# Leaving softmax rows undivided and multiplying the attention output by inverse row sums instead

## The chip, the cores and the metric

The kernel runs on one core of a Trainium2 chip. The metric is the device time of one execution in microseconds (us); lower is better. The engines are TensorE (PE in the profile; PEld is its weight load), VectorE (DVE), ScalarE (ACT), GpSimd (POOL) and SyncE (SP), which issues the DMA transfers.

## The reference

Three blocks in a row: an attention with a decay bias, a mixture of four experts with relu, and a gated feed-forward block.

```python
scores = (1 / sqrt(D)) * q @ k.T              # B=2, H=8, S=576, D=64
cum = cumsum(maximum(s, 0))
bias = -(cum[:, None] - cum[None, :])
scores = where(causal, -1e9, scores + minimum(bias, 0))
attn = exp(scores - max(scores))
attn = attn / (sum(attn) + 1e-9)
x = (attn @ v) as [1152, 512]                 # heads side by side
p = domain_probs / (sum(domain_probs) + 1e-9)
x = sum over e of p[:, e] * (maximum(x @ w1[e], 0) @ w2[e])      # 4 experts, F = 1024
g = x @ w_gate                                # F = 1536
out = ((g * sigmoid(g)) * (x @ w_val)) @ w_out
```

## The kernel before

**One program, ordered by a planner.** The Python code creates tasks (`add`, or `any_of` where one of several engines may do it) with an engine, an estimated cost, the tasks they depend on, a rank, and the buffers they take and give back (`Ring`). `Plan.step` takes again and again the ready task that can start first by these estimates, with the lower rank winning a tie, and writes its instructions down. So the order on each engine is fixed when the program is built, and each engine works through its own list in that order. A task that may run on several engines (letters `v`, `a`, `p` for DVE, ACT, POOL) goes to the one with the best estimated end.

**Attention.** A unit is a pair of heads and a group of query blocks of 128 rows: 16 pairs in all. The first eight pairs hold query blocks 0 and 1 and are computed in plain fp32 (four chains each); the last eight hold blocks 2, 3 and the half block 4, in split precision (five chains each, since block 4 has 64 rows and takes both heads at once). That makes 72 chains. A chain is:

- `scores` (tag `sp`): the score matmuls, line L599;
- `least`: mask and row minimum of the negated scores into the tile `ns`, on DVE, L608;
- `exp`: on ACT, L615, with the row sums as a by-product in column 2 of the small tile `st`;
- `guard`: two DVE instructions on 128x1, add 1e-9 (L620) and reciprocal (L621);
- `norm`: `ns` times the inverse sum, row by row, on POOL or DVE (L314, the body of `scale`);
- `turn`: TensorE transposes `ns` into the bank `tp`, L645; `copy`: ACT or DVE moves it to `p`, L304 or L306.

After the chains of a pair, `products` (L695) multiplies by v into the bank `po`, whose rows are the two heads' 64 dimensions and whose columns are tokens. `values` then writes `po` to `xh` (rounded, `high`) and the rest to `xl` (`low`, L711). There are five `ns` buffers, two `sp` banks, two `tp` banks and one `po` bank.

**What lies beside attention.** The four pairs with query blocks 0 and 1 of the first batch fill the first 256 tokens of x. As soon as they are done, the planner may also hand out the expert block ("dense" work): matmuls into the bank `h` (lines L1036 to L1038, three for each product in split precision), into `o` (L1196 to L1198), their evacuations on ACT and DVE, and the preparation of weights (a cast on ACT, `wah` or `woh`, and a subtraction on POOL, `wal` or `wol`, L317). While attention runs, a job covers 256 or 512 tokens of one expert's slice (`jobs`, list `part`), with eight products where the later form of the same work (`seven`, L1134 to L1136) needs seven. Where TensorE would have nothing in the estimate, a filler transposition is written (L404). The jobs handed out by the end of attention are all done in the plain form; the form with seven products begins after them, and its sums of x are made by `sums_of_x`.

## Time and profile before

| What | Before |
|---|---|
| Runs | 3976.26, 752.39 and 751.43 us (median 752.39) |
| Profiled execution | 750.75 us |
| Its span, first to last instruction | 748.9 us |
| Busy: PE, PEld | 722.3 us (96%), 628.7 us (84%) |
| Busy: DVE, ACT, POOL | 615.1 (82%), 374.8 (50%), 442.8 us (59%) |
| Mean granted TensorE clock, as a share of full | 0.995 |
| Last value product of attention (L695) | up to 156.5 us |
| First product in the form with seven (L1134) | 212.7 us |

The shares of a whole span hide the stages. Attention, alone or with early dense work beside it, fills the first 157 us; then come the rest of the early jobs, and from about 213 us the long stretch of expert and feed-forward products. In a timeline a matmul's duration includes its latency: the distance from one start to the next is what it costs TensorE in a row of them.

### The profile page before, as it was taken

To read this page: it belongs to the slowest core of one execution; us is meant where nothing else is said; L and a number is where in the kernel's file an instruction comes from. 1 tells how busy PE (TensorE), PEld (TensorE's weight loads), DVE (VectorE), ACT (ScalarE), POOL (GpSimd) and SP (SyncE) were. 2 spreads that over 40 slices of the span, in tenths; PEclk is the share of its full clock that TensorE was granted. 3 is DMA by queue.
4 is the path that set the end of the run, shared out by engine and by line. 5 is a ranking of instruction groups with operands and counts; after the bars stand their busy time and mean duration, and the time that the engine had idled before them with its cause. 6 is when DMAs were issued, how large, how long until landed. Compare 5 with 4: busy or idle time off the path is not lost.

```text
span 748.9 us, 12443 instructions
## 1 busy us (share of the span) xinstructions
PE 722.3 (96%) x4332; PEld 628.7 (84%) x4332; DVE 615.1 (82%) x1251; ACT 374.8 (50%) x845; POOL 442.8 (59%) x440
## 2 busy tenths in 40 slices
PE   7999999999999998999999999999899999999997
PEld 6767766778788897989889898899798999999996
DVE  7688886769988988889977989779897788787765
ACT  4999786845435454545635455365642423243210
POOL 5345543489744466655565574579886676676321
PEclk8999999999999999999999999999999999999999
DMA  5557532003454234442445344202210101010003
GB/s 115 122 134 213 153 93 58 29 1 113 155 188 166 91 136 144 141 157 92 141 141 169 93 155 134 99 29 93 77 57 29 57 30 57 29 57 1 1 1 126
DMA packets 77230, 72.57 MB, mean 97 GB/s; under 512 B 45976, under 2 KB 56280, under 8 KB 77168
## 3 DMA queue, kind: packets, MB, share of 16 engines
q1 hardware_dynamic: 77168, 71.78, 31.2%
q8 instruction: 34, 0.56, 0.3%
q14 instruction: 28, 0.23, 0.1%
HBM read 59.82 MB, written 11.80 MB: 96 GB/s over the span
## 4 chain that ended last, share of the span: by engine, by line
PE 64%; DVE 17%; DMA 7%; issue 5%; ACT 4%; SPq 1%; POOL 0%; DVEq 0%; POOLq 0%; ACTq 0%
PE h L1134 9%; PE h L1136 9%; PE h L1135 9%; PE o L1196 8%; PE o L1197 8%; PE o L1198 8%; DMA hh<-in_moe_w_val 3%; PE sp L599 3%; PE po L695 2%; PE tp L645 2%; DVE cc L1153 2%; DMA hh<-in_moe_w_out 2%; DVE hl L804 2%; DVE ns L608 2%; DMA hh<-in_moe_w_gate 1%
## 5 line engine op out<-in xcount | busy, mean ns | idle before, releaser
L1196 PE MATMUL o<-woh,hh 128*128 128x512 f32 x396 | 157.0, 396 | 5.3 <-DVE acc_b L1280 2.9
L1153 DVE TENSOR_TENSOR cc<-cc,h 128x320 f32<-128x320 f32 (+1 forms) x288 | 127.1, 450 | 38.6 <-PE h L1136 30.9
L1198 PE MATMUL o<-woh,hl 128*128 128x512 f32 x396 | 155.1, 392 | 3.0 <-POOL hl L317 1.9
L1197 PE MATMUL o<-wol,hh 128*128 128x512 f32 x396 | 155.8, 393 | 0.0
L317 POOL TENSOR_TENSOR wal<-raw,wah 128x512 fp32r<-128x512 f32 (+1 forms) x56 | 71.5, 1290 | 42.1 <-ACT wah L304 42.1
L1134 PE MATMUL h<-xh,wsh 128*128 128x320 f32 (+1 forms) x320 | 95.2, 298 | 0.7 <-ACT cc L304 0.7
L1136 PE MATMUL h<-xh,wsl 128*128 128x320 f32 (+1 forms) x320 | 95.0, 297 | 0.0
L1135 PE MATMUL h<-xl,wsh 128*128 128x320 f32 (+1 forms) x320 | 94.9, 297 | 0.0
L1198 PEld LDWEIGHTS o<-woh,hl 128*128 128x128 f32 x396 | 74.4, 188 | 21.2 <-POOL hl L317 2.8
L1196 PEld LDWEIGHTS o<-woh,hh 128*128 128x128 f32 x396 | 74.5, 188 | 19.8 <-DVE acc_b L1280 4.6
L317 POOL TENSOR_TENSOR hl<-cc,hh 128x512 fp32r<-128x512 f32 (+1 forms) x29 | 41.7, 1436 | 75.4 <-ACT hh L1256 70.1
L317 POOL TENSOR_TENSOR wol<-raw,woh 128x512 fp32r<-128x512 f32 x52 | 75.0, 1453 | 16.1 <-ACT woh L304 16.0
L1197 PEld LDWEIGHTS o<-wol,hh 128*128 128x128 f32 x396 | 74.5, 188 | 10.8
L1253 ACT ACTIVATE cc<-cc 128x640 f32<-128x640 f32 (+1 forms) x48 | 33.3, 694 | 99.6 <-DVE cc L1153 99.6
L314 POOL TENSOR_SCALAR ns<-ns,st 128x256 f32<-128x256 f32 (+4 forms) x62 | 33.6, 544 | 64.1 <-DVE st L621 14.5
L1134 PE MATMUL h<-xh,wah 128*128 128x256 f32 (+1 forms) x240 | 71.1, 296 | 0.0
L1136 PE MATMUL h<-xh,wal 128*128 128x256 f32 (+1 forms) x240 | 71.0, 296 | 0.0
L1135 PE MATMUL h<-xl,wah 128*128 128x256 f32 (+1 forms) x240 | 71.0, 296 | 0.0
L1134 PEld LDWEIGHTS h<-xh,wsh 128*128 128x128 f32 x320 | 60.4, 189 | 2.6 <-ACT cc L304 1.1
L1135 PEld LDWEIGHTS h<-xl,wsh 128*128 128x128 f32 x320 | 60.5, 189 | 1.4
L1136 PEld LDWEIGHTS h<-xh,wsl 128*128 128x128 f32 x320 | 60.5, 189 | 0.0
L1280 DVE SCALAR_TENSOR_TENSOR acc_b<-o,pr,acc_b 128x512 f32<-128x512 f32 x75 | 55.4, 742 | 5.1 <-PE o L1198 4.8
(156 smaller groups left out, 1823.0 us busy)
## 6 DMA issues: line engine op xcount, KB each, us to landing
raw<-in_moe_w SPq DMA_DIRECT2D x40, 512.0 KB
n<-hl SPq DMA_DIRECT2D x36, 256.0 KB
raw<-n SPq DMA_DIRECT2D x18, 512.0 KB
hh<-in_moe_w_gate SPq DMA_DIRECT2D x12, 512.0 KB
hh<-in_moe_w_val SPq DMA_DIRECT2D x12, 512.0 KB
hh<-in_moe_w_out SPq DMA_DIRECT2D x12, 512.0 KB
kr<-in_k SPq DMA_DIRECT2D x24, 128.0 KB
qr<-in_q SPq DMA_DIRECT2D x24, 128.0 KB
```

What stands on the lines that cost most here:

```text
L314: {"v": nc.vector, "p": nc.gpsimd}[e].tensor_scalar(to, x, by, 1.0, op0=ALU.mult, op1=ALU.mult)
L317: {"v": nc.vector, "p": nc.gpsimd}[e].tensor_tensor(to, x, f32(y), op=ALU.subtract)
L599: nc.tensor.matmul(sp[:, :s1 - s0], Q[:m, h, x0:x0 + P], K[:m, h, s0:s1], start=x == 0, stop=x == len(todo) - 1)
L1134: nc.tensor.matmul(hp, wh, h, start=c == 0, stop=False)
L1135: nc.tensor.matmul(hp, wh, l, start=False, stop=False)
L1136: nc.tensor.matmul(hp, wl, h, start=False, stop=c == 1)
L1153: nc.vector.tensor_tensor(part(k), part(x), banks[i], op=ALU.add)
L1196: nc.tensor.matmul(op, hh[:, f, ts], wh[:, f, :], start=f == 0, stop=False)
L1197: nc.tensor.matmul(op, hh[:, f, ts], wl[:, f, :], start=False, stop=False)
L1198: nc.tensor.matmul(op, hl[:, f, ts], wh[:, f, :], start=False, stop=f == NF - 1)
L1253: nc.scalar.activation(src()[:, o], src()[:, o], AF.Relu)
L1280: nc.vector.scalar_tensor_tensor(acc(t), bank_(), sc, acc(t), op0=ALU.mult, op1=ALU.add)
```

## The change

The rows of `ns` are no longer divided by their sums. `guard` and `norm` are gone from all 72 chains, and `turn` waits for `exp` alone. `exp` leaves its sum in a tile `sums` that a pair shares (a column for each chain). Once for each pair, two DVE instructions make the inverses of all columns (`inverse`); `spread` copies each column over 64 columns of a tile `inv_w` (POOL or DVE; 256 columns, and for the half block `spread_last` writes two 64x64 corners); `rows_of` turns `inv_w` on TensorE into a `tp` bank, so that the inverse of a token stands in its column for the 64 rows of its head (for the half block a matmul with `twin`, two identity halves added); `keep` copies this to a tile `R`; `product` multiplies the bank `po` by `R` into `R` on DVE; `high` and `low` make `xh` and `xl` from `R` instead of from `po`. There are four `ns` buffers in place of five. Besides, the tile `dps` is no longer there (`pr` is used), and the sums of x of the second half get a rank behind the preparation of the weights.

```diff
-NS = 5
+NS = 4
-NORM = "pv"
...
+        inv_w = ap.tile([P, 3, P], F32, name="inv_w", bufs=1)
+        twin = ap.tile([P, D], F32, name="twin", bufs=1)
+
+        def halves():
+            nc.gpsimd.memset(inv_w[:, 2], 0.0)
+            nc.gpsimd.tensor_tensor(twin, ident[:, :D], ident[:, D:], op=ALU.add)
+        t_own = add("pool", 0.6, halves, [t_id], rank=11)
...
-                box["st"] = ap.tile([P, 6], F32, name="st", tag="st", bufs=8)
+                box["st"] = ap.tile([P, 2], F32, name="st", tag="st", bufs=6)
...
-                    ns, ns, AF.Exp, bias=st[:, len(spans) - 1:len(spans)], scale=-1.0, accum_out=st[:, 2:3])
-
-            def guard():
-                st = box["st"]
-                nc.vector.tensor_scalar(st[:, 4:5], st[:, 2:3], 1.0e-9, None, op0=ALU.add)
-                nc.vector.reciprocal(st[:, 5:6], st[:, 4:5])
-
-            def norm(on):
-                ns = box["ns"][:, :w]
-                scale(on, ns, ns, box["st"][:, 5:6])
+                    ns, ns, AF.Exp, bias=st[:, len(spans) - 1:len(spans)], scale=-1.0, accum_out=ch.sum(qb, heads))
...
-            tG = inorder("g", add("dve", 0.21, guard, [tE, before.get("g")], rank=i + RANK["g"]))
-            tN = inorder("n", any_of(NORM, "scale", w, norm, [tG, before.get("n")], rank=i + RANK["n"]))
+            ch.exps.append(tE)
...
-                tT = inorder("t", add("pe", (c1 - c0) * pe(2 * P), turn, [tN, before.get("t")],
+                tT = inorder("t", add("pe", (c1 - c0) * pe(2 * P), turn, [tE, before.get("t")],
...
+                def inverse():
+                    m = 2 * nf + (nf < len(self.qbs))
+                    box["inv"] = self.sums[:, 1, :m]
+                    nc.vector.tensor_scalar(self.sums[:, 0, :m], self.sums[:, 0, :m], 1.0e-9, None, op0=ALU.add)
+                    nc.vector.reciprocal(box["inv"], self.sums[:, 0, :m])
+
+
+                def spread(on):
+                    to = inv_w[:, :nf].rearrange("p b (h d) -> p (b h) d", h=2)
+                    move(on, to, box["inv"][:, :2 * nf].unsqueeze(2).to_broadcast([P, 2 * nf, D]))
+
+                def spread_last(on):
+                    for x in half:
+                        move(on, inv_w[x, nf, x], box["inv"][x, 2 * nf:].to_broadcast([D, D]))
+
+                def rows_of():
+                    box["r"] = ps.tile([P, BANK], F32, name="tp", tag="tp", bufs=2)
+                    for x in range(len(self.qbs)):
+                        a, m = x * P, min(P, n - x * P)
+                        if m == P:
+                            nc.tensor.transpose(box["r"][:, a:a + m], inv_w[:, x], ident)
+                        else:
+                            nc.tensor.matmul(box["r"][:, a:a + m], inv_w[:, x], twin, start=True, stop=True)
+
+                def keep(on):
+                    box["R"] = ap.tile([P, 320], F32, name="R", tag="R", bufs=1)[:, :n]
+                    move(on, box["R"], box["r"][:, :n])
+
+                def product():
+                    nc.vector.tensor_tensor(box["R"], self.po[:, :n], box["R"], op=ALU.mult)
+
                 def high(on):
-                    move(on, xh[:, hp, dst], self.po[:, :n])
-
-                def low():
-                    nc.vector.tensor_tensor(xl[:, hp, dst], self.po[:, :n], f32(xh[:, hp, dst]), op=ALU.subtract)
+                    move(on, xh[:, hp, dst], box["R"])
+
+                def low(on):
+                    minus(on, xl[:, hp, dst], box["R"], xh[:, hp, dst])
+                r = i + RANK["f"]
+                tI = add("dve", 0.38, inverse, list(self.exps), rank=i + RANK["g"])
+                tW = [any_of("pv", "copy", 2 * nf * D, spread, [tI], take=[ring("iw", 1)], rank=i + RANK["g"])]
...
+                tR = inorder("t", add("pe", nf * pe(2 * P) + (len(self.qbs) - nf) * pe32(D), rows_of, tW + [before.get("t"), t_own],
+                                      take=[ring("tp")], give=[(tW[0], ring("iw"))], rank=i + RANK["g"]))
+                tK = any_of(COPY, "bank", n, keep, [tR], take=[ring("R", 1)], give=[(tR, ring("tp"))], rank=i + RANK["g"])
...
-                tX = any_of(FOLD, "bank", n, high, [tV], rank=i + RANK["f"])
-                done_x[g].append(add("dve", dve(n), low, [tX], give=[(tV, ring("po", 1))], rank=i + RANK["f"]))
+                tF = add("dve", dve(n), product, [tV, tK], give=[(tV, ring("po", 1))], rank=r)
+                tX = any_of("av", "copy", n, high, [tF], rank=r)
+                done_x[g].append(any_of("vp", "two", n, low, [tX], give=[(tK, ring("R"))], rank=r))
...
+        rank = WRANK + made["n"] - 2 if t0 else prompt() + 1
...
-        dps = ap.tile([P, NT, E], F32, name="dps", bufs=1)
+        dps = pr
```

The planner orders the changed program anew, and dense work moves. In TensorE's list the last value product stands behind 120 dense matmuls before the change and behind 162 after it; the jobs handed out by the end of attention are four before and six after. The first place is TensorE's list at the eighth pair, the last one in plain fp32 (`sp` scores, `tp` transposes of `ns`, `h` first transposes of k with `kr` and then dense products of `xh` and `wah`, `po` the value product). Before the change:

```order
L599 MATMUL sp<-kb_111,qb_115 128x64
L508 MATMUL h<-ident,kr 128x128 x4
L645 MATMUL tp<-ident,ns 128x128 x2
L1036 MATMUL h<-xh,wah 128x256
L1037 MATMUL h<-xl,wah 128x256
L1038 MATMUL h<-xh,wal 128x256
...
L695 MATMUL po<-p,vr 64x256 x2
L695 MATMUL po<-p,vr 64x128 x2
L645 MATMUL tp<-ident,ns 128x128 x3
```

After it, at the same pair (the lines have other numbers: L607 was L599, L516 was L508, L643 was L645, L700 was L695, L1248 to L1250 were L1196 to L1198; L737 is `rows_of`):

```order
L1248 MATMUL o<-woh,hh 128x512
L1249 MATMUL o<-wol,hh 128x512
L1250 MATMUL o<-woh,hl 128x512
...
L607 MATMUL sp<-kb_111,qb_115 128x64
L700 MATMUL po<-p,vr 64x256 x2
L700 MATMUL po<-p,vr 64x128 x2
L516 MATMUL h<-ident,kr 128x128 x4
...
L737 MATMUL tp<-ident,inv_w 128x128 x2
L643 MATMUL tp<-ident,ns 128x128 x3
```

Twelve dense matmuls, the four products of `h` just ahead, stand before this pair's value product before the change; after it there are 51, and the second matrix of the first job (`o`) has begun.

The second place is the end of attention on TensorE, the last pair, before the change:

```order
L1038 MATMUL h<-xh,wal 128x512
L645 MATMUL tp<-ident,ns 128x128 x7
L1196 MATMUL o<-woh,hh 128x512
L1197 MATMUL o<-wol,hh 128x512
L1198 MATMUL o<-woh,hl 128x512
...
L695 MATMUL po<-p,vr 64x320 x6
L695 MATMUL po<-p,vr 64x192 x2
L695 MATMUL po<-p,vr 64x64 x2
```

And after it:

```order
L643 MATMUL tp<-ident,ns 128x128 x7
L1248 MATMUL o<-woh,hh 128x512
L1249 MATMUL o<-wol,hh 128x512
L1250 MATMUL o<-woh,hl 128x512
L737 MATMUL tp<-ident,inv_w 128x128 x2
L739 MATMUL tp<-twin,inv_w 128x64
L700 MATMUL po<-p,vr 64x320 x6
L700 MATMUL po<-p,vr 64x192 x2
L700 MATMUL po<-p,vr 64x64 x2
```

`rows_of` now stands directly ahead of the value product. At four of the last eight pairs it stands ahead of it, here and at two others with nothing or one short block between; at the other four it stands behind it.

The third place is POOL's list, from the seventh pair on (`wal` and `wol` are the weight subtractions, `kb` a copy of k), before the change:

```order
L317 TENSOR_TENSOR wal<-raw,wah 128x512 x2
L314 TENSOR_SCALAR ns<-ns,st 128x256
L314 TENSOR_SCALAR ns<-ns,st 128x128
L314 TENSOR_SCALAR ns<-ns,st 128x256
L314 TENSOR_SCALAR ns<-ns,st 128x384
L308 TENSOR_SCALAR kb_113<-ka_112 64x512
```

And after it:

```order
L316 TENSOR_TENSOR wal<-raw,wah 128x512 x2
L316 TENSOR_TENSOR wol<-raw,woh 128x512 x2
L307 TENSOR_SCALAR inv_w<-sums 128x256
L316 TENSOR_TENSOR wal<-raw,wah 128x512 x2
L307 TENSOR_SCALAR kb_113<-ka_112 64x64
```

The multiplications of `ns` are gone, a spread stands where a pair ends, and the weight subtractions follow one another.

## Rows read from the trace of the kernel before

**Rows 1.** Windows by stretch: length, PE, PEld, DVE, ACT, POOL busy, clock, DMA, GB/s.

```profile
12.00:48.00 36.00, 34.22 (x216) 25.34 (x217) 23.71 (x140) 32.50 (x122) 14.29 (x30) 0.91 0.50 114
48.00:84.00 36.00, 33.95 (x235) 25.80 (x236) 32.92 (x113) 33.61 (x96) 19.88 (x25) 1.00 0.65 176
84.00:157.00 73.00, 69.89 (x433) 50.48 (x433) 50.95 (x176) 50.76 (x141) 32.61 (x44) 1.00 0.27 71
157.00:213.00 56.00, 54.46 (x272) 46.49 (x271) 54.78 (x77) 27.17 (x58) 44.01 (x41) 1.00 0.37 118
213.00:744.00 531.00, 521.34 (x3138) 472.71 (x3136) 441.83 (x732) 227.59 (x426) 324.39 (x276) 1.00 0.28 91
```

**Rows 2.** Chain of waits, shares by line, of 12 to 48, 48 to 84, 84 to 157 us.

```profile
by line: PE sp L599 30.0%; PE tp L645 14.8%; PE h L508 9.4%; PE po L695 8.9%; DMA dps<-in_moe_domain_probs 5.4%; PE o L404 4.2%; ACT ns L615 3.9%; issue 3.6%; DVE ns L608 3.5%; SPq L1522 3.3%; SPq L1520 2.7%; POOL ns L314 2.1%; SPq L450 1.8
...
by line: DVE ns L608 18.2%; DVE ka L551 9.5%; PE tp L645 8.4%; DVE ns L314 7.8%; DVE qb L554 7.2%; ACT ka L304 6.8%; PE po L695 6.5%; issue 5.7%; PE sp L599 4.2%; PE h L508 3.6%; ACT ns L615 3.5%; ACT wah L304 2.9%; DVE st L621 2.9%; DVE p 
...
by line: PE po L695 16.1%; PE sp L599 14.7%; PE tp L645 11.5%; PE h L508 6.1%; DVE ns L608 5.5%; PE h L1036 5.0%; PE h L1038 4.5%; PE h L1037 4.5%; ACT p L304 4.2%; PE o L1196 3.8%; ACT ns L615 3.8%; DVE ka L551 3.8%; PE o L1197 2.9%; PE o 
```

**Rows 3.** Groups by line and shape, 0 to 157 us: count, busy, mean, idle before.

```profile
L621 DVE RECIPROCAL st<-st 128x1 f32<-128x1 f32 x72 | 11.8, 164 | 2.5
L620 DVE TENSOR_SCALAR st<-st 128x1 f32<-128x1 f32 x72 | 10.7, 148 | 8.6 <-ACT ns L615 8.1
L304 ACT COPY p<-tp 128x256 f32<-128x256 f32 x30 | 10.4, 375 | 0.2
L314 POOL TENSOR_SCALAR ns<-ns,st 128x256 f32<-128x256 f32 x16 | 7.6, 478 | 15.3 <-DVE st L620 3.7 <-PE tp L645 3.0 <-ACT ns L615 2.8
L314 DVE TENSOR_SCALAR ns<-ns,st 128x512 f32<-128x512 f32 x6 | 5.3, 889 | 0.2
L304 ACT CAST xh<-po 128x320 fp32r<-128x320 f32 x8 | 3.4, 424 | 8.3 <-PE po L695 8.2
L304 ACT CAST xh<-po 128x256 fp32r<-128x256 f32 x7 | 2.6, 373 | 0.8 <-PE po L695 0.8
L317 POOL TENSOR_TENSOR wal<-raw,wah 128x512 fp32r<-128x512 f32 x10 | 12.7, 1279 | 2.6 <-ACT wah L304 2.6
```

**Rows 4.** Timeline of PE: products of 64 and of 256 columns, start and duration.

```profile
53.41 0.28 PE L599 MATMUL sp<-kb,qb 68*128 68x64 f32 x1
53.53 0.66 PE L508 MATMUL h<-ident,kr 128*128 128x128 f32 x4
...
54.59 0.28 PE L1036 MATMUL h<-xh,wah 128*128 128x256 f32 x1
54.71 0.28 PE L1037 MATMUL h<-xl,wah 128*128 128x256 f32 x1
```

**Rows 5.** Timeline of PE: dense products of 512 columns.

```profile
165.12 0.40 PE L1037 MATMUL h<-xl,wah 128*128 128x512 f32 x1
165.35 0.39 PE L1038 MATMUL h<-xh,wal 128*128 128x512 f32 x1
```

**Rows 6.** Chain of waits, pieces in time: a block of transposes, a value product.

```profile
142.34 0.77 PE tp L645 x7
144.41 2.35 PE po L695 x20
```

**Rows 7.** Timelines of DVE and of POOL around 65 us.

```profile
64.80 1.35 DVE L314 TENSOR_SCALAR ns<-ns,st 128x512 f32<-128x512 f32 x1
...
64.59 1.29 POOL L317 TENSOR_TENSOR wol<-raw,woh 128x512 fp32r<-128x512 f32 x1
```

**Rows 8.** Writers of the tile xl: min/median/max ns, first and last start.

```profile
L711 DVE TENSOR_TENSOR xl<-po,xh x16: 404/448/492, 23.0 to 157.0; 128x256 fp32r<-128x256 f32 x8, 128x320 fp32r<-128x320 f32 x8
...
L317 DVE TENSOR_TENSOR xl<-tt,xh x7: 406/768/1173, 162.9 to 545.0; 128x256 fp32r<-128x256 f32 x4, 128x320 fp32r<-128x320 f32 x3
```

**Rows 9.** Writers of the tiles mask and kb on POOL, in ns.

```profile
L308 POOL TENSOR_SCALAR mask<-mask x2: 453/612/770, 7.4 to 7.9; 64x64 f32<-64x64 f32 x2
...
L308 POOL TENSOR_SCALAR kb<-ka x12: 236/611/617, 55.0 to 137.5; 64x512 fp32r<-64x512 f32 x8, 64x64 fp32r<-64x64 f32 x4
```

**Rows 10.** Waits of 12 to 84 us: total, times, longest.

```profile
PEld tp L645 <- POOL ns L314: 4.2, 11, 1.3
```

More of the change, by code (lines that the diff above doesn't have):

```diff
@@ L676, in __init__, with sum @@
                 self.a, self.e = qbs[0] * P, min((qbs[-1] + 1) * P, S)
-                self.p, self.owner, self.done = {}, {}, {0: [], 1: []}
+                self.p, self.owner, self.done, self.exps, self.sums = {}, {}, {0: [], 1: []}, [], None
+            def sum(self, qb, heads):
+                if self.sums is None:
+                    self.sums = ap.tile([P, 2, 2 * len(self.qbs)], F32, name="sums", tag="sums", bufs=2)
+                x = 2 * (qb - self.qbs[0]) + heads[0]
+                return self.sums[:, 0, x:x + 1]
             def spot(self, t, c, lo, hi, kn):
@@ L705, in values @@
                 dst = slice(place[g], place[g] + n)
-                def high(on):
-                    move(on, xh[:, hp, dst], self.po[:, :n])
-                def low():
-                    nc.vector.tensor_tensor(xl[:, hp, dst], self.po[:, :n], f32(xh[:, hp, dst]), op=ALU.subtract)
+                box = {}
+                full = [qb for qb in self.qbs if rows(qb) == P]
+                nf = len(full)
+                def inverse():
[3 more added lines that the diff above has]
+                    nc.vector.reciprocal(box["inv"], self.sums[:, 0, :m])
@@ new lines, in values @@
+                tI = add("dve", 0.38, inverse, list(self.exps), rank=i + RANK["g"])
+                tW = [any_of("pv", "copy", 2 * nf * D, spread, [tI], take=[ring("iw", 1)], rank=i + RANK["g"])]
+                if nf < len(self.qbs):
+                    tW.append(any_of("pv", "copy", P, spread_last, [tI, t_own, tW[0]], n=2, rank=i + RANK["g"]))
+                tR = inorder("t", add("pe", nf * pe(2 * P) + (len(self.qbs) - nf) * pe32(D), rows_of, tW + [before.get("t"), t_own],
+                                      take=[ring("tp")], give=[(tW[0], ring("iw"))], rank=i + RANK["g"]))
@@ L1073, in run @@
                     {"v": nc.vector, "p": nc.gpsimd}[on].tensor_tensor(tmp[name][:, c], x_, y_, op=op)
-                return any_of(TADD, "two", n, run, at, take=[rg] if new and c == 0 else [], rank=prompt() + 1)
+                return any_of(TADD, "two", n, run, at, take=[rg] if new and c == 0 else [], rank=rank)
             first = task(0, deps[0])
@@ L1088, in low @@
                     minus(on, box["l"][:, i, c], tmp[name][:, c], box["h"][:, i, c])
-                hi = any_of(THIGH, "copy", n, high, [t[c]], rank=prompt() + 1)
-                done[i].append(any_of(TLOW, "two", n, low, [hi], rank=prompt() + 1))
+                hi = any_of(THIGH, "copy", n, high, [t[c]], rank=rank)
+                done[i].append(any_of(TLOW, "two", n, low, [hi], rank=rank))
             return done[i]
```

## The prediction

> **What bounds the kernel now.** I read the windows by stage first, then the chain of waits in each stage, then the groups by shape. From 213 us on TensorE is busy 521.3 of 531 us, and from 157 to 213 us 54.5 of 56 [rows 1]: there the time is the work that TensorE has, and nothing that DVE or POOL is spared buys time. The change acts in the first 157 us. These fall into three parts. From 12 to 48 us (plain fp32 pairs) ACT is busy 32.5 of 36 us and DVE only 23.7 [rows 1], and the chain runs mostly through TensorE's small matmuls [rows 2]. From 48 to 84 us ACT (33.6 of 36) and DVE (32.9) are both nearly full [rows 1], and DVE leads the chain [rows 2]. From 84 to 157 us DVE and ACT are at 51 of 73 us, TensorE at 69.9 [rows 1], and the chain is TensorE's again [rows 2]. TensorE's busy shares overstate it, since the duration of a lone matmul is mostly latency: a 256-column product lasts 0.28 us, but the next one starts 0.12 us later [rows 4]. So there is room on TensorE in attention, and the fillers (4.2% of the chain from 12 to 48 us) stand in some of it [rows 2].
>
> **Dense work comes earlier: -6.9 us.** By the two orders, 162 dense matmuls instead of 120 stand ahead of the last value product. The 42 are 24 of 256 columns and 18 of 512. A 256-column one costs 0.117 us from start to start, 0.12 rounded in the timeline [rows 4], a 512-column one 0.23 [rows 5]: 24 x 0.117 + 18 x 0.23 = 6.9 us that TensorE no longer has to do behind attention. This gain is real only if attention does not grow by it. By the orders, the surplus is there by the eighth pair (51 instead of 12) and complete by the tenth (87 instead of 36), in the time up to about 84 us, where TensorE is not the bound; behind that the dense work between the pairs is about the same. I count it whole; at worst it is paid back in full and the term is zero.
>
> **Two more jobs in the plain form: +1.3 us.** Six jobs instead of four are handed out early. They replace 84 products of 256 columns in the form with seven by 48 of 256 and 24 of 512. 48 x 0.117 + 24 x 0.23 - 84 x 0.117 = 11.1 - 9.8 = +1.3 us on TensorE [rows 4, 5]. It falls where TensorE is the bound, so it counts whole.
>
> **What DVE loses and gets.** It loses 144 guard instructions, 72 x (0.148 + 0.164) = 22.5 us, ten multiplications of `ns` (the six of 512 columns alone 5.3 us) [rows 3] and sixteen subtractions from `po` at a median of 0.45 us [rows 8], 7.2 us. It gets 32 instructions for the inverses at the price of the guards, 5.0 us; sixteen products of two operands with one in PSUM, which is the form of the old subtraction, 7.2 us; and 14 subtractions and 8 casts of `R`. The subtraction now has both sources in SBUF; the like of it took 0.41 to 1.17 us, median 0.77 [rows 8], so 14 x 0.77 = 10.8 us, bounds 5.7 and 16.4. On balance DVE has some 10 us less in attention. It pays only from 48 to 84 us, where DVE leads. There the chain has 7.8% in multiplications of `ns` and 2.9% in reciprocals [rows 2], 0.107 x 36 = 3.9 us. What comes late next is ACT, full to 33.6 of 36 us [rows 1], so no more than 2.4 us can be gained unless ACT is relieved too. I take -2.4, bounds 0 and -3.9.
>
> One multiplication of 512 columns on DVE ran from 64.80 for 1.35 us and ended 0.27 us after POOL's weight subtraction, which ran from 64.59 for 1.29 us; the mean of the six is 0.89 [rows 3, 7]. The Trainium skill (SBUF — State Buffer, section on the two separate sides) says that DVE and GpSimd share one pair of SBUF ports as an exclusive lock, taken by a DVE instruction in its fast one-source mode, or by one with two SBUF sources against a GpSimd instruction that reads SBUF. The trace agrees with it on the multiplication. The rule speaks against the change at one place: the new subtraction of `xh` from `R` has two SBUF sources, where the old one read PSUM, so by the rule it can be held up for a whole weight subtraction. With three pairs between 48 and 84 us and 1.28 us each that would be +3.8 us instead of the +1.0 that the medians 0.77 and 0.45 give; DVE's gain of that stretch would then be gone and the sum 2.4 us higher.
>
> **What ACT loses and gets: about 0.** In the plain pairs it gets 7 copies of `R` at the price of a `p` copy of the same shape, 0.375 us, and loses two casts of 0.373, three `p` copies and one copy of k, by the orders of instructions: 2.6 - 0.75 - 1.1 - 0.4 = +0.4 us [rows 3]. In the late pairs seven copies of `R` stand against five casts fewer. So ACT, which holds the pace up to 84 us, is not relieved. The two earlier pairs of weight casts that go with the earlier dense work lie on it too; I take nothing for them, and up to +3 us in the range.
>
> **What TensorE gets: +2.2 us.** For each pair two transposes and in the late pairs one product with `twin`, 32 + 8. Seven transposes took 0.77 us in a row [rows 6], 0.11 each; the 64-column product 0.12, by the nearest row [rows 4]. 40 x 0.11 = 4.4 us. About half of it falls into time in which TensorE waits or fills anyway: 2.2, bounds 0 and 4.4. What waits for them is the `tp` bank and behind it `turn` of the next pair.
>
> **What the chain loses elsewhere: -1.8 us.** Between `exp` and `turn` a chain had guard and `norm`, 0.31 + 0.48 us for 256 columns [rows 3], and TensorE's weight load waited for POOL's `norm` 11 times between 12 and 84 us, 4.2 us in all [rows 10]. Part of this was passed on to ACT-bound time. I take 2.1% of 36 us in the first stretch [rows 2] and 1 us behind 84 us, 1.8; bounds 0 and 4.2. That there are four `ns` buffers, not five, costs nothing as long as a buffer is held for a shorter time, which the missing steps see to. POOL's 62 multiplications go and 14 spreads come, at the price of its 256-column multiplication, 0.478 us [rows 3], and 16 corners of 0.24 to 0.77 us [rows 9], of which DVE does half; POOL is not on the chain, and the weights get ready sooner.
>
> **The sum.** -6.9 + 1.3 - 2.4 + 2.2 - 1.8 = -7.6 us on the profiled execution of 750.75 us, of which 748.9 is its span: 743.1. The two lower runs, 752.39 and 751.43, lie 1.2 us above the profiled one on average, so **744.3 us** is what I expect of a run, 1% below before. Runs cannot tell a change of under 2% (15 us) from none by the bound used for the chances.
>
> **Rivals.**
> (A) Attention stretches by what is put into it. ACT is full up to 84 us, and each early job brings its casts and relus there; then the 6.9 us move the end of attention back by as much, and DVE's relief is swallowed by ACT. The sum is 1.3 + 2.2 - 1.8 = +1.7, 753.5 us. For it: ACT's 33.6 of 36 us; against it: the new dense work stands where the old order had fillers and waits.
> (B) DVE's relief is worth more. If ACT's fullness from 12 to 84 us comes partly from waiting in turn with DVE, both run freer, and attention ends some 6 us earlier than forecast; with the extra dense work that gives 738. For it: the two engines alternate in the chain; against it: busy time is work done, and ACT has as much of it as before.
> (C) Slower: TensorE waits for `rows_of`. This needs exp, inverse on DVE, spread on POOL, and POOL's list has pairs of weight subtractions just ahead of spreads, 1.28 us each [rows 3]. TensorE takes its list in order, so every later transposition and score waits behind it. At half of the late pairs `rows_of` stands ahead of the value product. If a spread comes ready just behind two subtractions, 2.6 us are lost; at all eight late pairs 20 us, at six of them 15.4: 744.3 + 15.4 = 759.7. It decides as soon as the spread starts later than the last `turn` of the pair is copied. Against it: the old `norm` stood in the same queue 62 times, and TensorE lost only 4.2 us to it up to 84 us [rows 10].
> (D) The change does not do what it says: with the multiplications gone the chain shows the same waits under other names (`R`, `inv_w`), and only the jobs move: 744 to 753, inside the cases above.
>
> **Chances and range.** Forecast 0.48 (739 to 750); A with D 0.27 (750 to 756); B 0.15 (732 to 740); C 0.10 (755 to 770). Faster by over 2% means below 737.3: half of B and a little of the forecast, 0.09. Slower by over 2% means above 767.4: the far end of C, 0.03. The range of 735 to 757 leaves out the lower third of B, most of C and little else.
>
> **What the profile after would show.** The last value product should end between 151 and 158 us with 162 dense matmuls ahead of it; the first dense product should start near 40 us instead of 54.2; DVE should be some 10 us less busy up to there, ACT as before, POOL some 20 us less. In the stretch behind attention TensorE should have about 64 us of plain dense work, ahead of the first product in the form with seven. If TensorE waits for `inv_w` by more than 5 us in total, C is at work; if ACT is at 95% to the end of the tenth pair and the end of attention lies past 160 us, it is A. The forecast would be wrong altogether if the new order of the weights and sums of x behind 157 us opens waits on TensorE there, of which it has 1.5 us in 56 now [rows 1].

## The result and the profile after

The changed kernel takes **762.05 us** (median of four runs, 761.31 to 762.53) against 751.91 us for the kernel before in the same comparison. The ratio on record is 1.0116, 95% interval 1.0094 to 1.0138 (the quotient of the two medians is 1.0135). All ratios here are of fast runs: the 3976.26 us of the kernel before and two runs of b_ns4 below (761.03 and 762.63 us, at a lower clock) don't count in them. The changed kernel is 1.2% slower; 744.3 us was forecast, in a range up to 757. The profiled execution took 761.83 us with a span of 760.0, so 11.1 us of span have to be explained (748.9 before). The mean granted clock of its runs was 0.984 to 0.988; the profiled execution before had 0.995, and the other runs of that kernel, in the comparisons below, 0.989 to 0.997.

The windows of the changed kernel by stage, with the columns of [rows 1]:

```profile
12.00:48.00 36.00, 33.87 (x205) 26.87 (x206) 19.00 (x91) 30.03 (x111) 5.62 (x8) 0.82 0.56 126
48.00:84.00 36.00, 34.20 (x239) 27.19 (x237) 27.22 (x81) 31.52 (x93) 17.09 (x17) 1.00 0.76 192
84.00:157.00 73.00, 69.06 (x426) 51.16 (x425) 50.73 (x140) 53.48 (x153) 17.34 (x27) 0.98 0.27 71
157.00:213.00 56.00, 52.91 (x282) 42.66 (x280) 45.28 (x78) 27.98 (x67) 36.55 (x37) 1.00 0.18 57
213.00:744.00 531.00, 524.62 (x3121) 474.52 (x3122) 454.33 (x744) 233.75 (x438) 333.24 (x276) 0.99 0.30 96
```

DVE is spared much of what was forecast. From 12 to 84 us it is busy 46.2 us where it had 56.6 [rows 1], but by 84 us the changed kernel has done nine pairs and the one before ten. Summed over all of attention, the guards, multiplications, subtractions and casts that are gone took DVE 38.8 us, and what came in their place takes 31.0: 7.8 us less. POOL loses 33.7 us of multiplications and gets 9.1 us of spreads and subtractions. And yet attention is longer. The last value product in the timeline of TensorE:

```profile
169.77 2.42 PE L700 MATMUL po<-p,vr 128*64 128x320 f32 x20
```

It ends at 172.2 us, where the table of before has 156.5: 15.7 us later. Of these, 6.9 us are the 42 dense matmuls that now stand ahead of it (24 x 0.117 + 18 x 0.23). **The other 8.7 us are attention that got longer.** Some 3 of them go with TensorE's clock in this one execution (see the clock below), some 6 with the order. Idle engines don't show them: TensorE is busy in 69.1 of the 73 us from 84 to 157, as before. What happens is seen at one step from a late pair to the next, here the pair whose value product starts at 113.37. First ACT, then TensorE, then DVE and POOL of the changed kernel:

```profile
107.42 0.73 ACT L623 ACTIVATE ns<-ns,st 128x512 f32<-128x512 f32 x1
...
110.02 0.65 ACT L623 ACTIVATE ns<-ns,st 128x384 f32<-128x384 f32 x1
```

```profile
111.54 0.60 PE L643 MATMUL tp<-ident,ns 128*128 128x128 f32 x4
...
113.37 2.96 PE L700 MATMUL po<-p,vr 128*64 128x320 f32 x20
116.26 0.66 PE L516 MATMUL h<-ident,kr 128*128 128x128 f32 x4
116.67 0.42 PE L607 MATMUL sp<-ka,qa 128*128 128x384 f32 x1
...
117.57 0.38 PE L737 MATMUL tp<-ident,inv_w 128*128 128x128 f32 x2
117.79 0.33 PE L739 MATMUL tp<-twin,inv_w 128*128 128x64 f32 x2
117.96 0.50 PE L643 MATMUL tp<-ident,ns 128*128 128x128 f32 x3
```

```profile
111.63 1.44 DVE L305 COPY inv_w<-sums 64x64 f32<-64x64 f32 x2
...
117.31 0.56 DVE L616 CUSTOM_DVE_ANT_0 ns<-sp,mask 128x384 f32<-128x384 f32 x1 [2.35 <-PE sp L607]
```

```profile
111.32 0.41 POOL L307 TENSOR_SCALAR inv_w<-sums 128x256 f32<-128x256 f32 x1 [4.18 <-DVE sums L721]
111.73 2.52 POOL L316 TENSOR_TENSOR wol<-raw,woh 128x512 fp32r<-128x512 f32 x2
```

The last `exp` of the pair (512 columns) ends at 108.15, that of the next pair's first chain (384 columns) at 110.67. `inv_w` is complete at 113.07. But `rows_of` (L737, L739) starts at 117.57, behind the pair's value product and the next pair's scores, and directly behind it, at 117.96, comes the next pair's `turn`, 7.3 us after its `exp`. Meanwhile its `ns` stays occupied, and DVE waits 2.35 us for scores. At the first five late pairs `rows_of` starts 3.7 to 6.5 us after its spread is complete.

One step is not the mean. From the end of `exp` to the start of `turn` the 40 late chains take 3.45 us in the mean, against 3.34 before. The 32 chains of the first eight pairs take 3.04 against 1.92, and there `rows_of` starts 3.5 to 7.2 us after its spread from the fourth pair on. By the eighth pair's value product (end at 56.6 us before, 66.5 after, with 1.4 and 6.3 us of dense work ahead of it) 5.0 of the 8.7 us have come together.

### The profile page after: what moved, and what is told of

It is laid out like the page before. It is cut to its first block, busy times and chain, and to the rows that moved or that the text cites. A ratio compares the mean times of both kernels' runs of the same rounds, so it can differ in the third digit from the quotient of the medians.

```text
span 760.0 us, 12315 instructions
## 1 busy us (share of the span) xinstructions
PE 734.0 (97%) x4363; PEld 638.7 (84%) x4363; DVE 615.8 (81%) x1159; ACT 381.4 (50%) x866; POOL 421.5 (55%) x393
## 4 chain that ended last, share of the span: by engine, by line
PE 72%; DVE 14%; ACT 5%; issue 3%; DMA 3%; POOL 1%; SPq 0%; DVEq 0%; ACTq 0%
PE o L1248 10%; PE h L1186 9%; PE o L1249 9%; PE o L1250 9%; PE h L1188 9%; PE h L1187 9%; PE sp L607 4%; PE po L700 3%; PE tp L643 3%; DVE tt L1125 2%; DVE cc L1205 2%; PE h L516 2%; PE h L1086 1%; DVE acc_b L1332 1%; DMA hh<-in_moe_w_val 1%
## 5 line engine op out<-in xcount | busy, mean ns | idle before, releaser
L1248 PE MATMUL o<-woh,hh 128*128 128x512 f32 x396 | 158.9, 401 | 6.8 <-DVE acc_b L1332 3.5
L1250 PE MATMUL o<-woh,hl 128*128 128x512 f32 x396 | 155.8, 393 | 0.9 <-DVE hl L316 0.9
L1205 DVE TENSOR_TENSOR cc<-cc,h 128x320 f32<-128x320 f32 (+1 forms) x276 | 122.5, 452 | 33.8 <-PE h L1188 28.9
L316 POOL TENSOR_TENSOR wal<-raw,wah 128x512 fp32r<-128x512 f32 (+1 forms) x60 | 77.8, 1312 | 61.1 <-ACT wah L303 49.1
L316 POOL TENSOR_TENSOR wol<-raw,woh 128x512 fp32r<-128x512 f32 x56 | 82.5, 1485 | 28.9 <-ACT woh L303 28.8
L1248 PEld LDWEIGHTS o<-woh,hh 128*128 128x128 f32 x396 | 75.0, 189 | 22.9 <-DVE acc_b L1332 6.2
L1250 PEld LDWEIGHTS o<-woh,hl 128*128 128x128 f32 x396 | 75.0, 189 | 18.8 <-DVE hl L316 1.8
L1186 PE MATMUL h<-xh,wsh 128*128 128x320 f32 (+1 forms) x304 | 90.6, 298 | 0.1
L1188 PE MATMUL h<-xh,wsl 128*128 128x320 f32 (+1 forms) x304 | 90.5, 298 | 0.0
L1187 PE MATMUL h<-xl,wsh 128*128 128x320 f32 (+1 forms) x304 | 90.4, 297 | 0.0
L1188 PE MATMUL h<-xh,wal 128*128 128x256 f32 (+1 forms) x228 | 68.0, 298 | 0.0
L1187 PE MATMUL h<-xl,wah 128*128 128x256 f32 (+1 forms) x228 | 67.9, 298 | 0.0
L303 ACT CAST hh<-sg 128x512 fp32r<-128x512 f32 (+1 forms) x24 | 16.2, 676 | 85.2 <-POOL sg L1449 42.9
L1187 PEld LDWEIGHTS h<-xl,wsh 128*128 128x128 f32 x304 | 57.5, 189 | 1.3
L1188 PEld LDWEIGHTS h<-xh,wsl 128*128 128x128 f32 x304 | 57.4, 189 | 0.0
```

Of the source, the lines that this page charges most:

```text
L316: {"v": nc.vector, "p": nc.gpsimd}[e].tensor_tensor(to, x, f32(y), op=ALU.subtract)
L1186: nc.tensor.matmul(hp, wh, h, start=c == 0, stop=False)
L1187: nc.tensor.matmul(hp, wh, l, start=False, stop=False)
L1188: nc.tensor.matmul(hp, wl, h, start=False, stop=c == 1)
L1205: nc.vector.tensor_tensor(part(k), part(x), banks[i], op=ALU.add)
L1248: nc.tensor.matmul(op, hh[:, f, ts], wh[:, f, :], start=f == 0, stop=False)
```

## The experiments

Two theories stood first: that the dense work put into attention stretches it (theory 1), and that the new path is slower in itself (theory 2). In the table, "dense" is the work ahead of the last value product by TensorE's list, priced as in [rows 4, 5], and "net" is the end of the last value product less it; "half clock" is how long TensorE's granted clock stood at its lower level (1.2 GHz) up to there in that profile. Ratios are to the kernel before, run on the same chip.

| Kernel | Ratio, 95% interval | Last value product, us | Dense, us | Net, us | Half clock, us |
|---|---|---|---|---|---|
| before | 1 | 156.5 | 22.2 | 134.3 | 6.8 |
| after | 1.0116 [1.0094, 1.0138] | 172.2 | 29.2 | 143.0 | 17.1 |
| a_rank | 1.0124 [1.0099, 1.0149] | 169.3 | 29.2 | 140.1 | 10.2 |
| a_fill | 1.0093 [1.0070, 1.0115] | 166.9 | 29.2 | 137.7 | 3.4 |
| a_lastp | 1.0097 [1.0062, 1.0132] | 165.7 | 29.2 | 136.5 | 3.4 |
| a_late3 | 1.0056 [1.0038, 1.0075] | 163.7 | 22.2 | 141.5 | 13.7 |
| a_nodense | one run, 766.1 us | 150.8 | 0 | 150.8 | 13.7 |
| b_nodense | one run, 757.4 us | 136.7 | 0 | 136.7 | 10.2 |
| a_noin | 0.9972 [0.9945, 0.9999] | 145.3 | 12.5 | 132.8 | 6.8 |
| a_rowsv | 0.9970 [0.9952, 0.9988] | 148.3 | 12.5 | 135.8 | 13.7 |
| a_ns5 | 0.9989 [0.9966, 1.0012] | 148.4 | 13.2 | 135.2 | 13.7 |
| b_ns4 | 1.0022 [0.9995, 1.0049] | 155.4 | 20.9 | 134.5 | 10.2 |
| b_nodivp | 0.9971 [0.9952, 0.9991] | 137.8 | 7.0 | 130.8 | 10.2 |

Nets are best compared between rows with the same half clock: a_rank is 5.6 us longer than b_ns4, and a_late3 5.7 and 6.3 us longer than a_rowsv and a_ns5.

**No dense work, in both kernels: a_nodense, b_nodense.** Edit in both:

```diff
-            if all(x.end is not None for x in done_x[0]):
-                feed()
```

> The changed kernel with no dense work handed out until attention is over; nothing is left out. It shows attention by itself. Theory 1: its last value product ends no later than that of the kernel before under the same rule, 134 to 140 us, since DVE and POOL are relieved. Theory 2: it ends at least 5 us later than that one. The total says little, as the gaps of TensorE stay empty; 770 to 790.

> The kernel before with no dense work handed out until attention is over; nothing is left out. The other half of the comparison: by 156.5 us less 22 us of dense work its last value product should end at 134 to 142 us; the total at 765 to 785. Theory 1 expects it level with or later than the changed kernel under this rule, theory 2 at least 5 us earlier.

The last value products of the two, first of the changed kernel, then of the one before:

```profile
148.35 2.42 PE L700 MATMUL po<-p,vr 128*64 128x320 f32 x20
```

```profile
134.23 2.42 PE L695 MATMUL po<-p,vr 128*64 128x320 f32 x20
```

With no dense work at all the changed attention is 14.1 us longer. Here the first eight pairs are not to blame (they end at 56.7 and 57.5 us): the late ones take 11.8 us each against 9.9. So dense work is not the only cause, and theory 2 stands. The same numbers tell what dense work in attention costs: 22.2 us of it move the end by 19.8 us before (136.7 to 156.5), and 29.2 us move it by 21.4 us after. Most is paid for on the spot.

**Dense work as late as before: a_late3.** The changed kernel hands out dense work only when three pairs more are done, so that 120 dense matmuls stand ahead of the last value product.

```diff
-            if all(x.end is not None for x in done_x[0]):
+            if all(...) and sum(x.end is not None for x in done_x[1]) >= 3:
```

> The changed kernel, but dense work may be handed out only once seven pairs are done, so that 120 dense matmuls stand ahead of the last value product, as before the change (12 ahead of the eighth pair's). Theory 1, the dense work that came earlier pushed attention back: attention ends near 165 us instead of 172 and near the 156.5 of before plus a little, and the time is 752 to 755. Theory 2, the new way to the inverse rows is itself slower in attention by some 9 us: the last value product ends at 163 to 166 us with 7 us less dense work ahead of it, that work comes later, and the time stays at 759 to 763. Theory 3, the half-speed clock at the start: the same as theory 2 as long as two half-speed stretches show.

It gives back some 0.6% of the 1.2, and the net price of attention stays (141.5). Its 756.25 us lie between what theory 1 (752 to 755) and theory 2 (759 to 763) expected: about half of the loss goes with the dense work that comes earlier, the other half stays without it.

**The rank of the sums of x as before: a_rank** (`rank = prompt() + 1`) was the other part of the change that moves work.

> The changed kernel with the rank of the sums of x as before the change; attention's order stays as it is, word for word. Theories 1 and 2 place the loss inside attention and expect the same time within 3 us. If the new rank is at fault the time falls by more than 5 us; if it is what pays, the time rises.

Ratio 1.0124 [1.0099, 1.0149], 760.93 us: no part of the loss.

**The list of turns: a_noin.** `inorder` makes each step of a stage depend on the one before, and `rows_of` had been put into the stage of the turns.

```diff
-                tR = inorder("t", add("pe", ..., rows_of, tW + [before.get("t"), t_own], ...
+                tR = add("pe", ..., rows_of, tW + [before.get("t"), t_own], ...
```

> The changed kernel, but the step rows_of no longer stands in the in-order list of turns: it still comes after the turns of its own pair, but the next pair's turns need not wait for it. Nothing is left out of the computation. Theory P (the place of the new step: with the turn that waits for inverse and spread in the list, and a tp bank held until keep, the next pair's turns and with them the scores come late): 754 to 759 us, about 3 to 8 us below the changed kernel's 762; the last value product ends at 147 to 154 us with 78 instead of 162 dense matmuls ahead of it, and TensorE stands at fewer fillers in the late pairs. Theory Q (the price is the work itself: more instructions on TensorE and DVE held up beside POOL's subtractions): within 2 us of 762.

749.1 us, faster than theory P expected: the whole loss is gone with one word, though the planner now hands out only 78 dense matmuls ahead of the last value product. TensorE of this kernel at the same pair (the next pair's first `exp` ends at 97.13):

```profile
99.48 0.55 PE L643 MATMUL tp<-ident,ns 128*128 128x128 f32 x3
...
100.43 2.42 PE L700 MATMUL po<-p,vr 128*64 128x320 f32 x20
...
106.10 0.38 PE L737 MATMUL tp<-ident,inv_w 128*128 128x128 f32 x2
106.31 0.33 PE L739 MATMUL tp<-twin,inv_w 128*128 128x64 f32 x2
```

The next pair's `turn` comes 2.35 us after its `exp` and ahead of the value product; `rows_of` is as late as ever (6.7 us after its spread), and this costs nothing. In the mean of the first eight pairs `turn` now comes 1.22 us after `exp` instead of 3.04; in the late pairs 3.23 instead of 3.45, so there the one place says more than the mean. From 84 to 157 us TensorE is now nearly full (from 145 us on with dense work alone):

```profile
84.00:157.00 73.00, 72.46 (x472) 56.02 (x471) 52.16 (x146) 54.31 (x151) 33.23 (x48) 1.00 0.21 56
```

**Rank or bank: a_rowsv.** The list as in the changed kernel; only the rank of `rows_of` is another.

```diff
-                                      take=[ring("tp")], give=[(tW[0], ring("iw"))], rank=i + RANK["g"]))
+                                      take=[ring("tp")], give=[(tW[0], ring("iw"))], rank=i + RANK["v"]))
```

> The changed kernel with rows_of still in the in-order list of turns, but with the rank of the value product (-6) in place of its own (2.5); nothing else is changed and nothing left out. Theory R (rows_of is issued late because of its rank, behind the next pair's scores and its own pair's value product, and in the list it hands that lateness on to the next pair's turns, whose rank is -2): 748 to 752 us, as without the list, ratio 0.995 to 1.001, last value product at 144 to 149 us. Theory T (a tp bank held by a step that waits for inverse and spread is the price, whatever its rank): 756 to 762 us.

749.92 us, as without the list. In the late pairs `rows_of` now comes ahead of the value product, 0.3 to 3.7 us after its spread:

```profile
102.21 0.44 PE L737 MATMUL tp<-ident,inv_w 128*128 128x128 f32 x2
102.48 0.33 PE L739 MATMUL tp<-twin,inv_w 128*128 128x64 f32 x2
...
103.19 2.42 PE L700 MATMUL po<-p,vr 128*64 128x320 f32 x20
105.55 0.55 PE L643 MATMUL tp<-ident,ns 128*128 128x128 f32 x3
```

So the `tp` bank that a waiting step holds is not the price (theory T). The price is that a step of low urgency, rank 2.5, stands in a list whose other steps have rank -2. It hands its lateness on to the turns of the first eight pairs (1.93 us from `exp` to `turn` here, 3.04 in the changed kernel); for the late pairs (3.25 against 3.45) how it does so is not shown.

**The ns buffers: a_ns5 and b_ns4.** Five buffers in the changed kernel (`inv_w` and `R` lie in parts of `acc_a` that are idle until then), and four in the kernel before.

```diff
-NS = 4
+NS = 5
-        inv_w = ap.tile([P, 3, P], F32, name="inv_w", bufs=1)
+        inv_w = acc_a[:, 3, :3 * P].rearrange("p (b n) -> p b n", n=P)
-                    box["R"] = ap.tile([P, 320], F32, name="R", tag="R", bufs=1)[:, :n]
+                    box["R"] = acc_a[:, 2, :n]
```

> The changed kernel with five ns buffers as before the change instead of four; to make room, inv_w and R lie in two quarters of acc_a that nothing uses before the end of attention. Nothing is left out. Theory P with the buffers as its second half (a late turn holds its ns buffer, and with four of them the scores of the next pair stop): 755 to 759 us, last value product at 148 to 156 us. If the four buffers cost nothing, as the prediction had it: 762 within 1.5 us.

> The kernel before with four ns buffers instead of five, all else as it was. Theory P (four buffers hurt only where a turn comes late): 751 to 753.5 us, last value product within 2 us of 156.5 less what dense work moves behind it. If four buffers have a price of their own: 755 us or more.

A fifth buffer alone also takes the loss away (750.02 us), better than expected, though the late pairs' turns come even later (4.64 us from `exp` to `turn` in the mean, 3.45 in the changed kernel). Four buffers in the kernel before cost next to nothing: the interval of 1.0022 holds 1. So it takes both, `rows_of` at its place in the list and four buffers. That a late turn holds a buffer and so stops the next scores is seen in the first eight pairs (3.04 us from `exp` to `turn` after, 1.85 in b_ns4); in the late pairs the two are nearly alike (3.45 and 3.28), and there it stays argued.

A rival is that the planner drew a bad order by chance, and that any edit that makes it plan anew would help. Against it: three different edits, each planned anew, end within 1 us of each other (749.1, 749.9 and 750.0 us), while a_late3, also planned anew but with list, rank and buffers as they are, stays at 756.3. It is not excluded.

**What division costs at all: b_nodivp.** The kernel before without guard and norm, planned anew:

```diff
-            tG = inorder("g", add("dve", 0.21, guard, [tE, before.get("g")], rank=i + RANK["g"]))
-            tN = inorder("n", any_of(NORM, "scale", w, norm, [tG, before.get("n")], rank=i + RANK["n"]))
...
-                tT = inorder("t", add("pe", (c1 - c0) * pe(2 * P), turn, [tN, before.get("t")],
+                tT = inorder("t", add("pe", (c1 - c0) * pe(2 * P), turn, [tE, before.get("t")],
```

> The kernel before with guard and norm taken out and the order planned anew without them; the division is left out of the computation. It is the most that any cheaper way of dividing could bring. By the prediction's terms for guard, norm and DVE's relief (1.8 and 2.4 us, up to 8 with their upper bounds): 746 to 750 us. If these steps lay beside other work altogether: 750.5 to 752.

749.31 us: an attention that doesn't divide is 0.3% faster, about 2 us, and a_noin and a_rowsv win as much. It is not the upper bound that its expectation calls it, since this kernel too is planned anew: a_noin_lp and a_best below are at 0.994, though the intervals overlap.

**The corners on POOL: a_lastp and a_noin_lp.** The 64x64 copies of `spread_last` always go to POOL; about half had gone to DVE.

```diff
-                        move(on, inv_w[x, nf, x], ...
+                        move("p", inv_w[x, nf, x], ...
```

> The changed kernel in the same order on TensorE, ACT and SP; the two 64x64 corners of the spread always go to POOL, where before about half of them went to DVE. Nothing is left out. Theory L (a DVE copy of 64x64 that meets a POOL subtraction lasts 1.2 instead of 0.2 to 0.3 us, and TensorE waits for it): 759 to 760.5 us, and the waits of the rows_of matmuls on DVE's corners, 1.3 to 1.5 us each, are gone. If these waits are paid anyway by what else is late: 762 within 1 us.

> The kernel of a_noin with the 64x64 corners always on POOL, without the fillers of a_best. Nothing is left out. If the corners are what a_best gained over a_noin: ratio 0.993 to 0.995; if it was the fillers: 0.996 to 0.999.

Ratios 1.0097 [1.0062, 1.0132] for 1.0116, and 0.9944 [0.9914, 0.9973] for 0.9972: both times some 2 us less, a_lastp just faster than theory L's range, but the intervals overlap, and a_lastp also had the better clock (0.988 to 0.998, against 0.984 to 0.988). What the edit does is plain in the traces. Writers of `inv_w` in the changed kernel (ns, minimum, median, maximum), and then in a_lastp:

```profile
L307 POOL TENSOR_SCALAR inv_w<-sums x22: 236/406/453, 17.0 to 167.8; 128x256 f32<-128x256 f32 x14, 64x64 f32<-64x64 f32 x8
...
L305 DVE COPY inv_w<-sums x10: 181/300/1241, 23.4 to 167.9; 64x64 f32<-64x64 f32 x8, 128x256 f32<-128x256 f32 x2
```

```profile
L307 POOL TENSOR_SCALAR inv_w<-sums x30: 234/242/473, 16.6 to 162.0; 64x64 f32<-64x64 f32 x16, 128x256 f32<-128x256 f32 x14
```

**The clock: a_fill.** TensorE's clock stood at half (1.2 GHz) for 13.7 us near the start, where before it had been 6.8 us. The windows of the changed kernel and of the one before:

```profile
11.40:25.10 13.70, 13.11 (x52) 10.94 (x53) 6.60 (x33) 9.57 (x35) 1.14 (x2) 0.50 0.25 56
```

```profile
14.20:21.00 6.80, 6.80 (x29) 5.83 (x28) 3.13 (x20) 5.80 (x22) 1.89 (x5) 0.50 0.23 53
```

So a_fill writes sixteen more fillers ahead of the first scores:


```diff
-            nc.tensor.transpose(idle["p"][:, :P], ident, ident)
+            idle["n"] = idle.get("n", 0) + 1
+            for _ in range(3 if 25 < idle["n"] <= 33 else 1):
+                nc.tensor.transpose(idle["p"][:, :P], ident, ident)
```

> The changed kernel with 16 more fillers on TensorE ahead of its first scores (three in the place of one, eight times), all else in the same order. Nothing is left out. Theory K (part of the 10 us is the clock: the changed kernel's runs had a mean granted clock of 0.984 to 0.988, those before 0.989 to 0.997): mean clock 0.990 or more and 757 to 760 us. If the clock of the first 25 us has no price because TensorE waits there anyway: 762 within 1 us, whatever the clock.

Clock 0.989 to 0.995 and 758.54 us, in theory K's range, 1.0093 [1.0070, 1.0115], which overlaps with the changed kernel's interval: by itself it doesn't settle what the clock costs in a run. But it bounds it: the kernel before had 0.989 to 0.995 in the same comparison, and at that clock the changed order is still 0.9% slower. So the clock is not the main cause.

In the profiled executions its share can be seen, since a_rank and a_fill have attention in the changed kernel's order on every engine (a_fill with its 16 fillers). Their last value products:

```profile
166.88 2.42 PE L700 MATMUL po<-p,vr 128*64 128x320 f32 x20
```

```profile
164.45 2.42 PE L702 MATMUL po<-p,vr 128*64 128x320 f32 x20
```

They end at 169.3 and 166.9 us instead of 172.2, with 10.2 and 3.4 us at half clock up to there instead of 17.1. By a_rank, some 3 of the changed kernel's 8.7 us are the clock of its profiled execution (an estimate). Why it stood at half for longer is not told: the runs of a_rank range from 0.983 to 0.992.

**Together: a_best and a_best2.** a_noin with the corners on POOL and the fillers, and a_rowsv with the same.

> a_noin with the 64x64 corners always on POOL (as a_lastp) and 16 more fillers early (as a_fill). Nothing is left out. If the three effects add: 4 to 8 us below the kernel before, ratio 0.990 to 0.995. If the corners and the clock cost nothing once the turns are free: as a_noin, ratio 0.996 to 0.999.

> a_rowsv with the corners on POOL and 16 more fillers early. Nothing is left out. Theory R: as a_best, ratio 0.991 to 0.997. Theory T: 1.00 or more.

a_best: 746.79 us, 0.9942 [0.9924, 0.9961]. a_noin_lp has the same without the fillers, so these bring nothing that can be told. a_best2: 0.9965 [0.9940, 0.9989], with mean clocks of 0.992 to 0.999 where a_rowsv had 0.989 to 0.995, and no faster than that beyond what can be told. a_noin_lp and a_best are the fastest versions, 0.6% below the kernel before.

**A miss: a_noin_nd**, a_noin without dense work.

> The kernel of a_noin with no dense work handed out until attention is over, as in a_nodense. Nothing is left out of the computation. Theory P (the place of rows_of in the list of turns is what makes the late pairs 1.8 us longer): the eight late pairs take 9.8 to 10.4 us each, against 11.8 in a_nodense and 9.9 in b_nodense, and the last value product ends at 138 to 143 us instead of 150.8. If the new work itself is the price, it stays at 148 us or later.

764.3 us in one run. The last value product ended at 143.3 us, just outside, and the late pairs took 11.1 us each (8.8 in the last five, 16.4 in the second and third). In the third DVE stood in the corners; DVE and POOL there:

```profile
87.78 2.67 DVE L305 COPY inv_w<-sums 128x256 f32<-128x256 f32 x3
```

```profile
87.64 1.27 POOL L316 TENSOR_TENSOR wal<-raw,wah 128x512 fp32r<-128x512 f32 x1 [0.89 <-ACT wah L303]
88.88 1.32 POOL L316 TENSOR_TENSOR wol<-raw,woh 128x512 fp32r<-128x512 f32 x1
```

Three copies of `inv_w` (one of 128x256, two corners) lasted 2.67 us together and ended 0.25 us after the second subtraction. TensorE's clock was also at half from 92 to 99 us. So a free list doesn't help every pair, and of the 14.1 us between a_nodense and b_nodense it takes away 7.5; how much of the two bad ones is the corners and how much the order wasn't told apart.

## Why the prediction was wrong

**"Dense work comes earlier: -6.9 us" failed, and it carried the forecast.** I counted the 42 matmuls whole, because they stood where TensorE was not the bound. The runs show the opposite. With 120 dense matmuls ahead, as before, a_late3 takes 756.25 us; with 162 the same kernel takes 760.93 (a_rank, on the same chip) to 762.05. So for this term and the 1.3 of the plain jobs, -5.6 together, stands +4.7 to +5.8. The last value product moved from 163.7 us to 169.3 and 172.2, by 5.6 to 8.5 us for 6.9 us of work: it was paid back there, in full or nearly. The term's bound, zero at the worst, was too good as well; why more was lost than the 1.3 is not told apart. The fastest versions have 78 dense matmuls ahead of the last value product, not 162. What I read as a gain is better read as a symptom: the planner fills holes with what is ready, and a longer attention has more of them. That is argued, not measured by itself.

**"What waits for them is the tp bank and behind it turn of the next pair" was written and priced at nothing; here some 6 of the 8.7 us arose.** I had the dependency before me and counted 40 instructions, 2.2 us, instead of asking where the step stands in its list. a_noin and a_rowsv, each by one edit, show it: 749.1 and 749.9 us. The 6 us are the differences of net at the same half clock, 5.6 to 6.3; the forecast's terms for attention itself (2.2 - 2.4 - 1.8) had promised -2.0. The other 3 us go with the clock, for which the prediction had no term.

**"That there are four ns buffers, not five, costs nothing as long as a buffer is held for a shorter time"** was right in its condition, which failed: a buffer is not held shorter. From the end of `exp` to the start of `turn` it took 3.34 us in the mean of the 40 late chains before, guard and norm included, and 3.45 after, with these gone; in the first eight pairs 1.92 and 3.04. b_ns4 shows next to no price for four buffers in the order before, a_ns5 shows the fifth worth 1.3% in the changed one.

**"The chain loses -1.8" and DVE's relief -2.4:** DVE has 7.8 us less to do in attention, where some 10 were forecast; its copies of `inv_w`, 5.8 us, had been given no time. For the two terms together with all that attention pays for dividing, b_nodivp gives some 2 us. In the changed kernel none of it arrived; a_noin is faster by as much.

**Held up by the lock:** the prediction feared a whole weight subtraction for the new subtraction of `xh` from `R`. It fell on another step. Those 14 took a median of 0.49 us and once 1.39; the copies of 64x64 took up to 1.24 us instead of 0.18 beside POOL's subtractions. The Trainium skill (SBUF — State Buffer, section on the two separate sides) says of DVE instructions in a two-port mode that they and GpSimd shut each other out for a whole instruction. The trace agrees with it: the three slow corners of the changed kernel ended 0.04 to 0.05 us behind a subtraction of POOL. That they ran in such a mode no run shows.

**The rivals.** C came nearest, 759.7 us, in its number by luck, and its first half is what happened: TensorE takes its list in order, and all that stands behind `rows_of` waits. Its second half, a wait for the spread behind POOL, is small: the waits of TensorE for `inv_w` from 84 to 173 us are these, of a matmul and of its weight load at one place, around 140 us.

```profile
PE tp L739 <- DVE inv_w L305: 1.3, 1, 1.3
```

```profile
PEld tp L739 <- DVE inv_w L305: 1.5, 1, 1.5
```

So its sign of more than 5 us didn't appear: the lateness was written into the order, and a wait that the order has filled with other work leaves no idle time. Of A's two signs one appeared, the end of attention past 160 us; the other, ACT at 95%, did not (31.5 of 36 us from 48 to 84). Its thought that attention stretches by what is put into it is right for the dense work; its sum, 753.5 us, has no price for the order.

**The rest of the 11.1 us:** 8.7 of attention and the 1.3 forecast for two more jobs in plain form make 10.0. That 1.3 was not measured by itself, and the remaining 1.1 was not told apart. In it may be TensorE's waits for DVE's accumulations behind attention (1.5 us before, between 156.5 and 213 us; 2.8 after, between 172 and 216) and two short stretches at half clock, one around 213 and one around 530 us.

## What to carry to other kernels

When a step is put into an in-order list, look at what stands behind it in the list and not only at what it costs: a step of low priority in a list of urgent ones can make them late, and a planner hides that by filling the time. More background work ahead of the end of a stage can then be a sign that the stage got longer; the number to compare is the end of the stage less the background work in it, between executions at the same clock: one and the same order ended attention at 172.2 and at 169.3 us. And a buffer count that is free in one order need not be in another.

## What was unexpected of the hardware

A DVE copy of 64x64 elements took 0.18 us at the least and 1.2 us beside a POOL subtraction of 1.28 us; three copies in a row ended only after two such subtractions had. Here is also one value product of 20 matmuls in the changed kernel, which took 3.85 us instead of 2.42, in a stretch of 3.4 us at half clock behind a pause of TensorE:

```profile
140.57 0.43 PE L739 MATMUL tp<-twin,inv_w 128*128 128x64 f32 x2 [1.28 <-DVE inv_w L305]
...
141.62 3.85 PE L700 MATMUL po<-p,vr 128*64 128x320 f32 x20
```

```profile
141.10:144.50 3.40, 3.14 (x13) 1.57 (x15) 2.40 (x6) 2.12 (x6) 1.26 (x1) 0.50 0.34 117
```

The two later falls of the clock in that profile, but for its last microseconds, came with a pause too: at 212.8 us in a wait of 2.5 us for DVE's accumulation, and at 530.3 us just behind one of 1.8 us. In the half-clock stretch that followed there TensorE was busy throughout:

```profile
529.92 0.53 PE L1248 MATMUL o<-woh,hh 128*128 128x512 f32 x1 [1.80 <-DVE acc_b L1332]
```

```profile
530.30:533.70 3.40, 3.40 (x12) 3.01 (x11) 2.78 (x5) 1.46 (x4) 1.00 (x2) 0.51 0.20 77
```

Not every such pause does it: the kernel before waited 1.5 us for DVE's accumulation between 156.5 and 213 us, at full clock throughout.
